# Putting off GpSimd's output sums and softmax weights behind the last low part of a block's input

## The chip, the cores and the metric

The kernel runs on one core of a Trainium2 chip. The metric is the time of one execution on the device, in microseconds (us). The engines are named as in the profile: PE (TensorE) multiplies matrices, ACT (ScalarE), DVE (VectorE) and POOL (GpSimd) work element by element, SP (SyncE) issues the DMAs. Each engine runs its own instructions in the order in which the program issued them, and semaphores order the engines among each other.

## The reference, cut to what matters

The inputs are `x` (8 x 4096 x 192), `weight_gen` (8 x 4096 x 8 heads x 7 taps) and the two weights of a feed-forward layer, `w_in` (192 x 2048) and `w_out` (2048 x 192). All is float32.

```
w = softmax(weight_gen over the 7 taps)
a[s, head, g] = sum over k of w[s, head, k] * x[s - 6 + k, head, g]     (zeros ahead of the sequence)
h = a @ w_in
out = (h * cos(h)) @ w_out
```

So each token gets a weighted sum of its own row and the six rows ahead of it, and that goes through a feed-forward layer whose activation is h times cos(h).

## The kernel before, in words

The 32768 tokens lie as 256 rows on each of the 128 partitions. The work goes in 64 blocks of 4 rows of every partition, 512 tokens a block. One loop over rounds `i` drives everything: 8 rounds to a block (`NPAIR`), and in each one pair of 128-wide chunks of the 2048 hidden columns. A float32 operand is split into a high part, which the matmul takes in its fast float32 form, and a low part in bfloat16, so that several cheap products replace an exact one.

What a round holds, engine by engine:

- PE, in this order: `ffn_in_first(i)` (line 484; the first of its matmuls reads `x_lo` of the block), `ffn_out(i - 6)` (line 625; the output product of an older block, 6 rounds behind), inside it `transpose_row` (lines 457 to 464; it turns one row of `xa` two blocks ahead and lets the result ride in free columns of the output's bank), and `ffn_in_second(i)` (line 503).
- ACT and DVE: for the hidden pair of the round before, ACT takes the whole turns (line 513), DVE the fraction (517), ACT the cosine (521), DVE the product h cos(h) (528); ACT and DVE then split it into high and low parts (539, 545). In every other round ACT copies the output bank to `part` (`evacuate`, line 650).
- POOL: the attention of a later block, as 13 steps: 7 products of x with the weights (`pr` or `xa`, line 356) and 6 sums (`xa`, line 372). The loop issues two steps at the end of a round (three in some rounds below 64). Block b starts when its weights are marked ready and block b - 2 has been transposed, both as the program is issued. Beside it POOL does the softmax's larger parts (lines 217 to 220, 294 to 309), the output sums (lines 666 and 667) and the low part of the transposed input (`split`, line 441).

Rounds are counted here by their remainder by 16, since the softmax works on 8 rows, which is two blocks, and repeats after 16 rounds. Of the block that is computed in rounds 8 to 15 the four rows are transposed in rounds 14 and 15, 0 and 1, 2 and 3, 4 and 5 ahead of it, and in the same way in rounds 6 to 13 for the block of rounds 0 to 7 that follow. After each second round ACT copies `part`, and the next round starts with `split`: ACT makes `x_hi` and `x_b` (437, 440), POOL `x_lo`. So `x_lo` of the last row is issued in round 6 (or 14) and PE reads it first at the start of round 8 (or 0).

The output of a block has two halves of the hidden columns and, in each, two pairs of token tiles (`tp` 0 and 1). The first half's `part` waits in `sums`. When the second half's is copied, in round 3 or 11 for `tp` 0 and in round 5 or 13 for `tp` 1, POOL adds the two (line 666, `part`) and then the two 192-wide columns of the result (line 667, `fin`). `finish` registers the DMA of `fin`, which SP issues three rounds later. SP also carries `traded`, a marker between PE's two groups of products in a round: PE's second group waits for it.

A table `later` holds what is put off: `at(when, do)` appends a call to a round, and the round runs its list after its products and ahead of POOL's attention steps. The softmax writes itself into it: subtraction of the maximum and the exponentials' sums in round 1, the reciprocal of the denominator on DVE in round 4, `weights` (line 300, 128 x 448) in round 5, every 16 rounds.

Of the kernel before, what the change touches and what calls it, by code (L numbers as in the profile page):

```python
# [17 lines left out]
ALU = mybir.AluOpType  # L18
# [26 lines left out]
def tile_softmax_conv_then_cos_ffn(  # L45
# [10 lines left out]
    B, S, D = x.shape  # L56
# [15 lines left out]
    LAG = 6  # L72
# [141 lines left out]
    def add_taps(t, out):  # L214
        three_ = work.tile([P, RW * H, 3], F32, name="three", bufs=1)
        three = three_[:, 0:t.shape[1]]
        nc.gpsimd.tensor_tensor(out=three, in0=t[:, :, 0:3], in1=t[:, :, 3:6], op=ALU.add)
        old = three[:, :, 0]
        for more in (three[:, :, 1], three[:, :, 2], t[:, :, 6]):
            nc.gpsimd.tensor_tensor(out=out, in0=old, in1=more, op=ALU.add)  # L220
            old = out
# [43 lines left out]
    PIECES = 8  # L265
    later = {}

    def softmax_later(i, r0, r1):

        n = (r1 - r0) * H  # L270
        tile_ = work.tile([P, RW * H, K], F32, name="taps")
        top = work.tile([P, RW * H], F32, name="top")
        den = work.tile([P, RW * H], F32, name="den")
        nc.sync.dma_start(out=tile_[:, 0:n].rearrange("p a k -> p (a k)"),
                          in_=g_v[:, :, r0 * H * K:r1 * H * K])
        for b in range(r0 // R, r1 // R):
            taps[b] = tile_.rearrange("p (r h) k -> p r h k", h=H)[:, b * R - r0:(b + 1) * R - r0]

        def at(when, do):
            later.setdefault(i + when, []).append(do)  # L280

        def half(start, c0, c1):
            m = c1 - c0
            t, m1, d = tile_[:, c0:c1], top[:, c0:c1], den[:, c0:c1]
            flat = t.rearrange("p a k -> p (a k)")
            step = m * K // PIECES
            num = []

            def numerators():
                num.append(work.tile([P, RW * H // 2, K], F32, name="num", bufs=1)[:, 0:m])  # L290
                nc.scalar.activation(out=num[0], in_=t, func=AF.Silu, bias=-SHIFT, scale=1.0)

            def exponentials():
                nc.gpsimd.tensor_tensor(out=t, in0=t, in1=num[0], op=ALU.mult)
                add_taps(t, d)
                nc.gpsimd.tensor_scalar(out=d, in0=d, scalar1=-1e-9 * math.exp(-SHIFT), scalar2=TWO_PI,
                                        op0=ALU.add, op1=ALU.mult)

            def weights():
                nc.gpsimd.tensor_tensor(  # L300
                    out=t, in0=t, in1=d.unsqueeze(2).broadcast_to([P, m, K]), op=ALU.mult)
                ready.update(range((r0 + c0 // H) // R, (r0 + c1 // H) // R))

            def piece(k):
                cs = slice(k * step, (k + 1) * step)
                nc.vector.reciprocal(out=flat[:, cs], in_=flat[:, cs])

            at(start, lambda: nc.vector.tensor_reduce(out=m1, in_=t, axis=AX.X, op=ALU.max))
            at(start + 1, lambda: nc.gpsimd.tensor_tensor(
                out=t, in0=t, in1=m1.unsqueeze(2).broadcast_to([P, m, K]), op=ALU.subtract))  # L310
            at(start + 4, numerators)
            at(start + 8, lambda: nc.scalar.activation(out=t, in_=t, func=AF.Silu, bias=SHIFT, scale=-1.0))
            for k in range(PIECES):
                at(start + 9 + k, lambda k=k: piece(k))
            at(start + 9 + PIECES, exponentials)
            at(start + 12 + PIECES, lambda: nc.vector.reciprocal(out=d, in_=d))
            at(start + 13 + PIECES, weights)

        for k, c0 in enumerate(range(0, n, RW * H // 2)):
            half(2 + 16 * k, c0, min(c0 + RW * H // 2, n))  # L320
# [114 lines left out]
    def split(b, t, cs, eng):  # L435
        hi, half, lo = parts_of(b)
        nc.scalar.copy(out=hi[:, :, cs], in_=t)  # L437
        yield
        if eng is nc.gpsimd:
            nc.scalar.copy(out=half[:, :, cs], in_=t)  # L440
        eng.tensor_tensor(  # L441
            out=lo[:, :, cs], in0=t, in1=hi[:, :, cs].bitcast(F32), op=ALU.subtract)
        if eng is not nc.gpsimd:
            yield
            nc.scalar.copy(out=half[:, :, cs], in_=hi[:, :, cs].bitcast(F32))  # L445
# [122 lines left out]
    def evacuate_f32(j):  # L568
        b, m = divmod(j, 2 * R)
        half, m = divmod(m, R)  # L570
        tp, bank = divmod(m, 2)
        if bank == 0:
            return
        acc = accs.pop(j // 2)
        part_ = work.tile([P, 2, CT], F32, name=f"part{half}", bufs=(3 if half == 0 else 2))
        part = part_[:, :, 0:D]
        nc.scalar.copy(out=part, in_=acc[:, :, 0:D])
        if half == 0:
            sums[(b, tp)] = part
            return  # L580
        if tp == 0:
            fin_t = work.tile([P, R, D], F32, name="fin")
            finals[b] = fin_t
        fin = finals[b]
        ts = slice(2 * tp, 2 * tp + 2)
        nc.gpsimd.tensor_tensor(out=fin[:, ts, :], in0=part, in1=sums.pop((b, tp)), op=ALU.add)
        finish(j, b, fin, tp)

    def finish(j, b, fin, tp):
        if tp == 1:  # L590
            def store():
                nc.sync.dma_start(out=o_v[:, :, b * R * D:(b + 1) * R * D],
                                  in_=fin.rearrange("p r d -> p (r d)"))

            stores[j + LATE] = store
            finals.pop(b)
            for pair in range(NPAIR):
                g_parts.pop(b * NPAIR + pair)
# [38 lines left out]
    def evacuate(j):  # L637
        if j < NATIVE:
            return evacuate_f32(j)
        b, m = divmod(j, 2 * R)  # L640
        half, m = divmod(m, R)
        tp, s = divmod(m, 2)
        if s == 0:
            return
        group = j // 2
        acc = accs.pop(group)
        bt = group // R + 2
        part = work.tile([P, 2, CT], F32, name=f"part{half}", bufs=(3 if half == 0 else 2))
        if WHOLE < bt < NB:
            nc.scalar.copy(out=part, in_=acc)  # L650
            r = group % R
            splits.append(split(bt, part[:, :, 2 * D:], slice(r * P, (r + 1) * P), nc.gpsimd))
        else:
            nc.scalar.copy(out=part[:, :, 0:2 * D], in_=acc[:, :, 0:2 * D])
        part = part[:, :, 0:2 * D]
        if half == 0:
            sums[(b, tp)] = part
            return
        if tp == 0:
            fin_t = work.tile([P, R, D], F32, name="fin")  # L660
            finals[b] = fin_t
        fin = finals[b]
        old = sums.pop((b, tp))
        eng = nc.gpsimd
        ts = slice(2 * tp, 2 * tp + 2)
        eng.tensor_tensor(out=part, in0=part, in1=old, op=ALU.add)  # L666
        eng.tensor_tensor(out=fin[:, ts, :], in0=part[:, :, 0:D], in1=part[:, :, D:2 * D],  # L667
                          op=ALU.add)
        finish(j, b, fin, tp)

    def last_half():
# [102 lines left out]
    for n in range(2):  # L774
        nc.tensor.matmul(warm[:, n, :], lhsT=ident, rhs=mix_last[0].rearrange("p r d -> p (r d)")[:, 0:CT],
                         start=True, stop=True, skip_group_check=True)
# [31 lines left out]
    for i in range(N + LAG + 1):  # L808
        b, pair = divmod(i, NPAIR)
        j = i - LAG  # L810
# [17 lines left out]
        def products():  # L828
            if b < NB and pair == 0:
                assert b in transposed  # L830
            if whole is not None and j >= 0:

                ffn_out(j)
                ffn_in_first(i, whole)
            elif j >= N - HALF:
                if j == N - HALF:
                    last_half()
                return
            else:
                if i < N:  # L840
                    ffn_in_first(i, h_now if whole is None else whole)
                if i == LAG:
                    ffn_in_second(i)
                if j >= 0:
                    ffn_out(j)
            if i < N and i != LAG:
                ffn_in_second(i)
            if j in stores:
                stores.pop(j)()
            if j >= 0:  # L850
                evacuate(j)
# [95 lines left out]
```

## Time and profile before

| What | Value |
| --- | --- |
| time, median of 3 runs | 2207.09 us (2206.64 to 2210.22) |
| time of the profiled execution | 2209.54 us |
| its span, first to last instruction | 2207.8 us |
| busy: PE, POOL, DVE, ACT | 98%, 92%, 89%, 86% |
| granted TensorE clock, mean | 0.997 |
| POOL's output sums, line 666 and line 667 | 124 each |
| POOL's weights, line 300, 128 x 448 | 28 |

The span is shorter than the time by what lies ahead of the first and behind the last instruction. In rows of the timeline stand the start, the duration, the engine, the line, the operation with its operands, how many instructions are merged and, in brackets, how long the engine was idle just before and what released it. In rows of the waits stand the waiting engine and line, the releaser, the total in us, the count and the longest. Instructions of one engine can overlap by some hundredths, so distances between starts are used for sums.

### The profile page before, as it was taken

The numbers are of one execution on the slowest core, as the hardware profiler recorded it, in microseconds if no ns is written. First come the engines' busy times: TensorE is split into PE (matmuls) and PEld (weight loads), VectorE is DVE, ScalarE is ACT, GpSimd is POOL, SyncE is SP. The second block draws the span as 40 slices with busy tenths as digits, with TensorE's granted clock in tenths as the row PEclk, the third lists the DMA queues.
The fourth block names the chain that finished last, engine by engine and source line by source line (L and its number), as shares of the span: only waits on it lengthen the run. The fifth ranks groups of instructions, "written<-read, shape, count | busy, mean of one in ns | idle before, by whom it ended". The sixth has DMA issues, their size and how long they took to land.

```text
span 2207.8 us, 60871 instructions
## 1 busy us (share of the span) xinstructions
PE 2154.1 (98%) x26428; PEld 1718.4 (78%) x26428; DVE 1973.9 (89%) x1876; ACT 1904.0 (86%) x2380; POOL 2033.8 (92%) x1587
## 2 busy tenths in 40 slices
PE   6999999999999999999999999999999999999998
PEld 3777787777877777877778787778777777778887
DVE  7788999989999899999989998999998899988887
ACT  6788888888888888888888888888888888888886
POOL 8999999999999999999999999999999999999941
PEclk9999999999999999999999999999999999999999
DMA  7312212112122121122121221221211212212100
GB/s 182 70 27 52 53 34 60 34 44 60 27 60 52 35 51 45 42 52 48 38 52 38 49 60 27 52 55 32 60 44 35 59 37 50 52 29 52 34 9 23
DMA packets 25914, 105.56 MB, mean 48 GB/s; under 512 B 2750, under 2 KB 6838, under 8 KB 25646
## 3 DMA queue, kind: packets, MB, share of 16 engines
q1 hardware_dynamic: 25646, 101.67, 19.5%
q8 instruction: 206, 3.38, 0.7%
q14 instruction: 62, 0.51, 0.1%
HBM read 76.50 MB, written 25.17 MB: 46 GB/s over the span
## 4 chain that ended last, share of the span: by engine, by line
POOL 54%; ACT 16%; PE 15%; DVE 10%; issue 4%; DMA 0%; POOLq 0%; ACTq 0%; SPq 0%; DVEq 0%
POOL xa L372 14%; POOL pr L356 14%; POOL part L666 7%; PE acc L625 7%; DVE turn L517 5%; PE h L503 5%; ACT turn L521 5%; POOL xa L356 4%; POOL fin L667 4%; ACT part L650 4%; ACT turn L513 4%; POOL x_lo L441 4%; DVE h L528 3%; PE h L484 3%; ACT ghi L539 2%
## 5 line engine op out<-in xcount | busy, mean ns | idle before, releaser
L625 PE MATMUL acc<-wo,ghi 64*128 64x384 f32 x7984 | 792.7, 335 | 0.4 <-ACT part L650 0.3
L517 DVE TENSOR_TENSOR turn<-h,turn 128x1024 f32<-128x1024 f32 x512 | 626.3, 1223 | 185.2 <-ACT turn L513 185.1
L625 PEld LDWEIGHTS acc<-wo,ghi 64*128 64x128 f32 x7984 | 721.6, 185 | 35.2 <-ACT part L650 10.9
L372 POOL TENSOR_TENSOR xa<-xa,pr 128x768 f32<-128x768 f32 (+1 forms) x378 | 690.2, 1826 | 0.6
L513 ACT ACTIVATE turn<-h 128x1024 int32<-128x1024 f32 x512 | 526.5, 1028 | 154.7 <-PE h L503 149.7
L521 ACT ACTIVATE turn<-turn 128x1024 f32<-128x1024 f32 x512 | 545.8, 1066 | 117.2 <-DVE turn L517 117.1
L528 DVE SCALAR_TENSOR_TENSOR h<-h,turn 128x1024 f32<-128x1024 f32 x504 | 621.1, 1232 | 28.0 <-ACT turn L521 1.1
L545 DVE TENSOR_TENSOR glo<-h,ghi 128x1024 bf16<-128x1024 f32 x504 | 611.7, 1214 | 2.9 <-POOL wo L204 1.7
L356 POOL TENSOR_TENSOR pr<-xt,taps 128x768 f32<-128x768 f32 (+1 forms) x378 | 579.0, 1532 | 8.8
L539 ACT CAST ghi<-h 128x1024 fp32r<-128x1024 f32 x504 | 510.8, 1013 | 1.9 <-DVE h L528 1.9
L625 PE MATMUL acc<-wo_b,glo 64*128 64x192 bf16 x7856 | 409.6, 243 | 0.0
L625 PEld LDWEIGHTS <-glo 64*128 64x128 bf16 x7984 | 327.2, 94 | 15.1 <-issue 2.4
L666 POOL TENSOR_TENSOR part<-part,part 128x768 f32<-128x768 f32 x124 | 229.2, 1848 | 90.9 <-ACT part L650 64.9
L484 PE MATMUL h<-x_hi,wa_hi 64*128 64x512 f32 x1024 | 303.0, 579 | 1.4 <-ACT x_hi L437 1.4
L503 PE MATMUL h<-x_hi,wa_hi 64*128 64x512 f32 x1024 | 302.6, 579 | 0.1
L650 ACT COPY part<-acc 128x1024 f32<-128x1024 f32 x240 | 239.2, 997 | 0.0
L484 PE MATMUL h<-x_lo,wa_hi 64*128 64x512 bf16 x1024 | 205.1, 388 | 27.0 <-POOL x_lo L441 23.7
L503 PE MATMUL h<-x_hi,wb_hi 64*128 64x512 f32 x1024 | 207.6, 394 | 0.0
L484 PE MATMUL h<-x_b,wa_lo 64*128 64x512 bf16 x1024 | 199.3, 377 | 1.9 <-ACT x_b L445 1.0
L503 PE MATMUL h<-x_lo,wa_hi 64*128 64x512 bf16 x1024 | 199.4, 378 | 0.8
L503 PE MATMUL h<-x_b,wa_lo 64*128 64x512 bf16 x1024 | 199.2, 377 | 0.0
L503 PE MATMUL h<-x_b,wb_lo 64*128 64x512 bf16 x1024 | 199.1, 377 | 0.0
(105 smaller groups left out, 2172.4 us busy)
## 6 DMA issues: line engine op xcount, KB each, us to landing
xt<-in_x_dram SPq DMA_DIRECT2D x62, 960.0 KB, 7.0
out_dram<-fin SPq DMA_DIRECT2D x63, 384.0 KB, 3.4
taps<-in_weight_gen_dram SPq DMA_DIRECT2D x15, 448.0 KB, 4.5
raw<-in_moe_w_out_dram SPq DMA_DIRECT2D x8, 384.0 KB, 4.9
raw<-in_moe_w_in_dram SPq DMA_DIRECT2D x10, 256.0 KB, 7.4
xt<-in_x_dram SPq DMA_DIRECT2D x1, 768.0 KB, 11.5
xt<-in_x_dram SPq DMA_DIRECT2D x1, 540.0 KB, 5.6
raw<-in_moe_w_in_dram SPq DMA_DIRECT2D x4, 128.0 KB, 4.9
```

What stands on the lines that cost most here:

```text
L356: eng.tensor_tensor(out=dst.rearrange("p r (h g) -> p r h g", h=H), in0=xt[:, k + ra:k + rb, :].rearrange("p r (h g) -> p r h g", h=H), in ...
L372: eng.tensor_tensor(out=acc if k < K else xa, in0=acc, in1=old[:, ra:rb], op=ALU.add)
L484: nc.tensor.matmul(h[:, q, :], lhsT=w[rs, chunk(pair, q)], rhs=v[rs, q, :], start=(m == 0), stop=False, skip_group_check=True)
L503: nc.tensor.matmul(h[:, 1 - q, :], lhsT=w[rs, cs], rhs=v[rs, q ^ middle, :], start=False, stop=(m == len(prods) - 1), skip_group_check=True)
L513: nc.scalar.activation(out=t.bitcast(I32), in_=hs[i], func=AF.Identity, bias=0.25, scale=1.0)
L517: nc.vector.tensor_tensor(out=t, in0=hs[i], in1=t.bitcast(I32), op=ALU.subtract)
L521: nc.scalar.activation(out=t, in_=t, func=AF.Sin, bias=SIN_BIAS, scale=SIN_SCALE)
L528: nc.vector.scalar_tensor_tensor(out=g, in0=hs[i], scalar=TWO_PI, in1=turns.pop(i), op0=ALU.mult, op1=ALU.mult)
L539: nc.scalar.copy(out=hi, in_=hs[i])
L545: nc.vector.tensor_tensor(out=lo, in0=hs.pop(i), in1=hi.bitcast(F32), op=ALU.subtract)
L625: nc.tensor.matmul(to, lhsT=g[rs, n, t * P:(t + 1) * P], rhs=w[rs, fc, :], start=(lo == 0 and c == 0 and (whole or s == 0)), stop=(lo == 1 ...
L666: eng.tensor_tensor(out=part, in0=part, in1=old, op=ALU.add)
```

## The change

POOL's two sums for `tp` 1 are no longer issued in the round that copies `part` (round 5 or 13) but through `later` two rounds on (round 7 or 15); those for `tp` 0 stay. The softmax's `weights` move from round 5 to round 6. Nothing is computed otherwise. The DMA of `fin` stays where it was, three rounds behind the copy.

```diff
             at(start + 9 + PIECES, exponentials)
             at(start + 12 + PIECES, lambda: nc.vector.reciprocal(out=d, in_=d))
-            at(start + 13 + PIECES, weights)
+            at(start + 14 + PIECES, weights)
...
         old = sums.pop((b, tp))
         eng = nc.gpsimd
         ts = slice(2 * tp, 2 * tp + 2)
-        eng.tensor_tensor(out=part, in0=part, in1=old, op=ALU.add)
-        eng.tensor_tensor(out=fin[:, ts, :], in0=part[:, :, 0:D], in1=part[:, :, D:2 * D],
-                          op=ALU.add)
+        def add():
+            eng.tensor_tensor(out=part, in0=part, in1=old, op=ALU.add)
+            eng.tensor_tensor(out=fin[:, ts, :], in0=part[:, :, 0:D], in1=part[:, :, D:2 * D],
+                              op=ALU.add)
+        if tp == 1:
+            later.setdefault(j + LAG + 2, []).append(add)
+        else:
+            add()
         finish(j, b, fin, tp)
```

## Prediction, made before the change was run

> **What bounds the kernel now.** I read the page's shares first, then the list of waits, then the timeline around one of the waits that carry the change, and last the rest of its 16 rounds. The fences stand in that order; rounds are counted by their remainder by 16.
>
> ```profile
> PE 2154.1 (98%) x26428; PEld 1718.4 (78%) x26428; DVE 1973.9 (89%) x1876; ACT 1904.0 (86%) x2380; POOL 2033.8 (92%) x1587
> POOL 54%; ACT 16%; PE 15%; DVE 10%; issue 4%; DMA 0%; POOLq 0%; ACTq 0%; SPq 0%; DVEq 0%
> ```
>
> PE is busy nearly throughout, so only its few waits can be won. Yet the chain that ended last lies on POOL for 54%: something of POOL's holds PE.
>
> ```profile
> POOL part L666 <- ACT part L650: 64.9, 33, 5.4
> PE h L484 <- POOL x_lo L441: 23.7, 28, 1.1
> PEld L484 <- DVE glo L545: 7.1, 22, 1.7
> PEld acc L462 <- POOL xa L372: 2.2, 1, 2.2
> ```
>
> The second row is PE's longest wait after the start, and its count, 28, is that of POOL's full-sized weights: one in 16 rounds. The first shows POOL idle at other places, 33 times: it is late at one place and early at another. The last, a wait of the transposes for an unfinished `xa`, has happened once; it comes back below. Now the place, PE's first matmul of rounds 5 to 8, with round 5's second group in between:
>
> ```profile
> 1000.88 0.39 PE L484 MATMUL h<-x_lo,wa_hi 64*128 64x512 bf16 x2
> 1003.67 0.38 PE L503 MATMUL h<-x_lo,wa_hi 64*128 64x512 bf16 x2
> 1005.00 0.39 PE L484 MATMUL h<-x_lo,wa_hi 64*128 64x512 bf16 x2
> ...
> 1009.14 0.39 PE L484 MATMUL h<-x_lo,wa_hi 64*128 64x512 bf16 x2
> ...
> 1014.28 0.39 PE L484 MATMUL h<-x_lo,wa_hi 64*128 64x512 bf16 x2 [0.85 <-POOL x_lo L441]
> ```
>
> Rounds 5 and 6 last 4.12 and 4.14 us, round 7 lasts 5.14: the wait of 0.85 costs 1.01 against a round of 4.13, since matmuls that otherwise overlap across the border are drained too. What held `x_lo` back (POOL), and when its input was there (ACT):
>
> ```profile
> 1004.36 0.99 ACT L650 COPY part<-acc 128x1024 f32<-128x1024 f32 x1
> 1005.86 0.74 POOL L441 TENSOR_TENSOR x_lo<-part,x_hi 128x256 bf16<-128x256 f32 x1
> 1006.56 1.83 POOL L666 TENSOR_TENSOR part<-part,part 128x768 f32<-128x768 f32 x1
> 1007.06 0.42 ACT L437 CAST x_hi<-part 128x256 fp32r<-128x256 f32 x1
> 1008.47 1.01 POOL L667 TENSOR_TENSOR fin<-part 128x384 f32<-128x384 f32 x1
> 1009.44 0.98 POOL L300 TENSOR_TENSOR taps<-taps,den 128x448 f32<-128x448 f32 x1
> 1010.50 1.55 POOL L356 TENSOR_TENSOR xa<-xt,taps 128x768 f32<-128x768 f32 x1
> 1012.00 1.54 POOL L356 TENSOR_TENSOR pr<-xt,taps 128x768 f32<-128x768 f32 x1
> 1013.50 0.73 POOL L441 TENSOR_TENSOR x_lo<-part,x_hi 128x256 bf16<-128x256 f32 x1
> 1014.19 1.55 POOL L356 TENSOR_TENSOR pr<-xt,taps 128x768 f32<-128x768 f32 x1
> 1015.69 1.84 POOL L372 TENSOR_TENSOR xa<-xa,pr 128x768 f32<-128x768 f32 x1
> 1017.61 1.54 POOL L356 TENSOR_TENSOR pr<-xt,taps 128x768 f32<-128x768 f32 x1
> ```
>
> The last row's `x_hi` is there at 1007.06 + 0.42 = 1007.48, but `x_lo` starts at 1013.50, ends at 1014.23, and PE starts 0.05 later. POOL was never idle in between: its queue held the two sums (2.88 from start to start of what follows), the weights (1.06) and two products (3.00).
>
> **The change part by part.** *The wait.* All that stood ahead of `x_lo` in round 5 goes: the sums to round 7, the weights to round 6, and the two products too. A block's attention starts when its weights are marked ready, in program order, and that is now round 6; in round 5 the loop issues no step. So `x_lo` follows the row before it (at POOL's idle time from 1006.56 on) and waits for `x_hi` alone. The delay from ACT's end to POOL's start I take as 0.08, from POOL's next wait for ACT, in the fence below: the copy ends at 1038.43 + 1.00, the sum starts at 1039.51. Then `x_lo` runs at 1007.56 to 1008.3, and PE wants it at 1013.27 (1009.14 + 4.13): 5.0 us in hand. Worth 28 x 1.01 = 28.3 us; the lower bound is the waits alone, 23.7.
>
> *The queue behind.* POOL's work is the same, only later, so the question is who waits for what now comes behind `x_lo`. Moved there are the weights 1.06, two products 3.00 and the sums 2.88: 6.94 in all. `x_lo` itself starts 1013.50 - 1007.56 = 5.94 earlier. So what POOL has left then runs 1.00 later than before, while PE's rounds come 1.01 earlier. The cover is POOL's idle time, and the rows that show it are these:
>
> ```profile
> 1032.35 1.85 POOL L666 TENSOR_TENSOR part<-part,part 128x768 f32<-128x768 f32 x1
> ...
> 1035.24 1.86 POOL L372 TENSOR_TENSOR xa<-xa,pr 128x768 f32<-128x768 f32 x1
> 1037.05 0.74 POOL L441 TENSOR_TENSOR x_lo<-part,x_hi 128x256 bf16<-128x256 f32 x1
> 1038.43 1.00 ACT L650 COPY part<-acc 128x1024 f32<-128x1024 f32 x1
> 1039.51 1.85 POOL L666 TENSOR_TENSOR part<-part,part 128x768 f32<-128x768 f32 x1 [1.71 <-ACT part L650]
> ...
> 1071.36 1.84 POOL L372 TENSOR_TENSOR xa<-xa,pr 128x768 f32<-128x768 f32 x1
> ```
>
> At 1039.51 POOL waited 1.71 for the copy that its sum of `tp` 1 needs. In the new order no sum stands there, and this idle time becomes work.
>
> *The transposes, the new tight place.* PE transposes the first row of `xa` 1.92 us into round 6 or 14 and needs the attention's last sum by then:
>
> ```profile
> 1006.92 0.14 PEld L462 LDWEIGHTS acc<-ident,xa 64*128 64x128 f32 x2
> ...
> 1039.07 0.41 PE L484 MATMUL h<-x_lo,wa_hi 64*128 64x512 bf16 x2
> ...
> 1072.37 0.39 PE L484 MATMUL h<-x_lo,wa_hi 64*128 64x512 bf16 x2
> ```
>
> In round 14 (1039.07): the attention started one round late, so its last sum moves from round 11 to round 12, behind the row's `x_lo`. Before it ended at 1037.10, that is 23.60 after the `x_lo` of 1013.50. Now it comes after those 23.60, the 6.94, one more `x_lo` (0.69, 1013.50 to 1014.19) and a wait of 0.31 for the copy of round 11, in all 31.54 behind 1007.56: 1039.10. The wait: that copy stood two rounds ahead of the one at 1038.43, so it ended at 1031.17, now 1030.16, and POOL may go on at 1030.24. POOL arrives at 1007.56, plus the 18.85 from 1013.50 to this sum at 1032.35, plus weights and sums 3.94, less 0.42 because two products (3.00) now stand for a product and a sum (1014.19 to 1017.61): 1029.93, 0.31 too early. PE transposes at 1039.07 - 1.01 + 1.92 = 1039.98. 0.9 us in hand.
>
> In the next round 6 (1072.37) the last sum now ends at 1071.36 + 1.84, less 5.94, plus 6.94, less the idle 1.71, plus the wait of 0.31: 1072.80. PE transposes at 1072.37 - 1.01 + 1.92 = 1073.28. 0.5 us in hand (before: 1.1). So I cost both at nothing, and name the price if the cover is gone: each 0.1 us beyond it is 2.8 us over 28 periods.
>
> *Does POOL's work still fit?* A period of 16 rounds:
>
> ```profile
> 1047.34:1114.63 67.29, 66.50 (x834) 53.33 (x833) 61.30 (x59) 59.20 (x75) 64.48 (x51) 1.00 0.19 43
> 1055.61 0.40 PE L484 MATMUL h<-x_lo,wa_hi 64*128 64x512 bf16 x2
> 1059.96 0.39 PE L484 MATMUL h<-x_lo,wa_hi 64*128 64x512 bf16 x2
> ```
>
> Without its idle 1.71 POOL needs 67.3 - 1.71 = 65.6, gaps between instructions included. PE's 16 rounds would last 67.3 - 1.01 = 66.3. 0.7 is left, of which the two waits named (for `x_hi` in round 6, for the copy in round 11) take a part. POOL will be busy almost throughout and still not bind. Round 2, at 1055.61, lasts 4.35, 0.22 too long: that is a wait for DVE's `glo` (22 of them, row above), after DVE's reciprocals, and I leave it in.
>
> *SP's queue.* The store of `fin` stays three rounds behind the copy, so it has one round behind the sums in place of three.
>
> ```profile
> 1017.41 0.59 SPq L592 DMA_DIRECT2D out_dram<-fin  x1
> ...
> 1050.43 0.59 SPq L592 DMA_DIRECT2D out_dram<-fin  x1
> ```
>
> The sums end at 1007.56 + 0.69 + 1.06 + 3.00 + 2.9 = 1015.2 in round 7 and, by the same counting from 1039.10 (two products, `x_lo`, a product and a sum, the sums), at 1049.1 in round 15. The stores come at 1016.4 and 1049.4 (1.01 earlier than before). Both are free to go, the second by 0.3. Behind it in SP's queue stands the marker that PE's second group of the next round waits for, and that group starts 2.8 into a round (1003.67 less 1000.88), about 3.8 after the store: a store some us late costs nothing either.
>
> *What else moves.* The weights one round later leave the reciprocal of round 4 further behind, at no cost. `part` and `fin` are held two rounds longer; their buffers come round after 8 rounds or more. The x load goes with the attention's steps, one round later, with five rounds before its first reader. At nothing, all of them.
>
> *A rule against it.* POOL's idle time shrinks, so its work meets more of DVE's. POOL's output sum and DVE's reciprocal as they are:
>
> ```profile
> L666 POOL TENSOR_TENSOR part<-part,part x124: 1807/1849/1882, 119.9 to 2180.5; 128x768 f32<-128x768 f32 x124
> L306 DVE RECIPROCAL taps<-taps x232: 316/493/496, 147.4 to 2061.5; 128x56 f32<-128x56 f32 x112, 128x28 f32<-128x28 f32 x4
> ```
>
> Least and most differ by 4% for the sum, and the reciprocal's median is its most but for 3 ns: neither is stretched by what the other does, so the sum stands. The Trainium skill, SBUF — State Buffer, section "Who interferes with whom", says that some DVE forms and POOL take a shared pair of ports by an exclusive lock, the other blocking for the whole instruction. If it bit here, a blocked piece would wait up to a sum's 1.85; the steady durations say that it does not.
>
> **Sum.** 28 x 1.01 = 28.3 less nothing. The profiled execution took 2209.5 around a span of 2207.8, which becomes 2179.5; the median of the runs, 2207.1, stands 0.1% below that execution. From the median: 2178.8, said as 2179.
>
> **The rivals.** *The wait moves to the transposes in part.* For: 0.5 and 0.9 us are small against 30 us of summed queue, and the same wait is in the list once. Against: each term is a row of the same loop and repeats. With 0.5 too late, 28 x 0.5 = 14 us come back: 2193. Still faster.
>
> *All of it comes back elsewhere: no change.* The stall gave ACT and DVE a rest of 1.01 every 16 rounds, just ahead of the reciprocals' rounds. If they need it, PE waits that long later, 2207. Against it: DVE had caught up before the stall, idle in round 7:
>
> ```profile
> 1010.40 1.23 DVE L517 TENSOR_TENSOR turn<-h,turn 128x1024 f32<-128x1024 f32 x1 [0.39 <-ACT turn L513]
> ```
>
> *Slower: the attention's start slips by another round.* If the steps come to be issued ahead of the weights, they start in round 7, and the last sum in round 14 stands two steps (3.4 us) later: 3.4 - 0.9 = 2.5 of wait for 1.01 won, 28 x 1.5 = 42 us more, 2249. It decides from 0.9 + 1.0 = 1.9 us of delay there, or 1.5 in round 6. Against: the round runs its list ahead of the steps. The Trainium skill, TensorE: Matmul & The Clock Gate, section "Why this matters for your kernels", adds that idle gaps over some 3 us drop the clock; no wait in these rows is as long.
>
> *The change does not do what it says*, `x_lo` held by something else: its only other input came 5.8 us before PE's need, so I give that nothing of its own.
>
> **How the numbers follow.** Full gain 0.70 (2175 to 2184), in part 0.17 (2184 to 2202), no change 0.07, slower 0.06. The range: down to 2173 if the 22 waits of 0.2 to 0.3 vanish too (28.3 + about 6), up to 2195 for a wait of 0.5 to 0.6 at the transposes. Bounded by 0.2% (4.4 us), about what a measurement here can tell from no change: faster 0.87, same 0.07, slower 0.06.
>
> **What would show it.** In the changed profile PE's wait for `x_lo` is gone and round 7 lasts 4.13; POOL's idle ahead of the sum in round 13 is gone; POOL waits some tenths for `x_hi` in round 6, 28 times; its busy share rises to 93%; PE's wait for `xa` stays at one. I am wrong if that last one appears some 28 times, if round 2 grows beyond 4.35, or if SP's wait for `fin` shows behind PE's second group.

## Result and the profile after

The changed kernel takes 2180.91 us (median of 4 runs, 2179.65 to 2181.82) against 2207.98 (2206.64 to 2210.22) for the kernel before: ratio 0.9876, 95% interval 0.9859 to 0.9893. The prediction said 2179, between 2173 and 2195. The kernel before has one run more here than above, so its median moved by 0.9.

The shares, the chain that ended last and the waits after, in the order in which they were shown of before. Lines behind the change have moved by one: the sums are now 667 and 668.

```profile
PE 2147.9 (99%) x26428; PEld 1676.9 (77%) x26428; DVE 1974.5 (91%) x1876; ACT 1903.5 (87%) x2380; POOL 2030.0 (93%) x1587
PE 95%; POOL 2%; DVE 1%; ACT 1%; DMA 0%; issue 0%; SPq 0%; DVEq 0%; ACTq 0%; POOLq 0%
```

```profile
POOL x_lo L441 <- ACT x_hi L437: 45.0, 34, 7.5
POOL part L667 <- ACT part L650: 14.0, 28, 5.4
PEld L484 <- DVE glo L545: 9.3, 29, 1.7
PEld acc L462 <- POOL xa L372: 2.1, 1, 2.1
```

The chain lay on POOL for 54%; now it lies on PE for 95%. PE's wait for `x_lo` has left the list, and POOL waits for `x_hi` in its place: what stood at the end of a queue now stands at its head. The wait of the transposes for `xa` is still one. The same place in the timeline, PE's rounds 6, 7 and 8 and POOL's queue:

```profile
990.84 0.39 PE L484 MATMUL h<-x_lo,wa_hi 64*128 64x512 bf16 x2
993.40 0.73 POOL L441 TENSOR_TENSOR x_lo<-part,x_hi 128x256 bf16<-128x256 f32 x1 [0.70 <-ACT x_hi L437]
994.09 0.97 POOL L300 TENSOR_TENSOR taps<-taps,den 128x448 f32<-128x448 f32 x1
994.97 0.39 PE L484 MATMUL h<-x_lo,wa_hi 64*128 64x512 bf16 x2
...
998.15 1.84 POOL L667 TENSOR_TENSOR part<-part,part 128x768 f32<-128x768 f32 x1
999.10 0.39 PE L484 MATMUL h<-x_lo,wa_hi 64*128 64x512 bf16 x2
```

Round 7 lasts 999.10 - 994.97 = 4.13 in place of 5.14. `x_lo` ends at 994.13, 5.0 ahead of PE. Behind it come the weights, the two products (left out in the fence) and the sums, in the predicted order. A whole period of 16 rounds; the row has its length, the busy time of PE, PEld (PE's weight loads), DVE, ACT and POOL with their instructions, then the granted clock, the DMA share and GB/s:

```profile
965.86:1032.17 66.31, 66.31 (x834) 52.04 (x833) 61.30 (x59) 59.20 (x75) 64.40 (x51) 1.00 0.21 50
```

66.31 in place of 67.29. PE counts as busy in all of it, though its round 2 is still 0.2 too long (below).

### The profile page after: what moved, and what is told of

Read it like the earlier page. It is cut to its first block, busy times and chain, and to the rows that moved or that the text cites. A ratio compares the mean times of both kernels' runs of the same rounds, so it can differ in the third digit from the quotient of the medians.

```text
span 2177.9 us, 60870 instructions
## 1 busy us (share of the span) xinstructions
PE 2147.9 (99%) x26428; PEld 1676.9 (77%) x26428; DVE 1974.5 (91%) x1876; ACT 1903.5 (87%) x2380; POOL 2030.0 (93%) x1587
## 4 chain that ended last, share of the span: by engine, by line
PE 95%; POOL 2%; DVE 1%; ACT 1%; DMA 0%; issue 0%; SPq 0%; DVEq 0%; ACTq 0%; POOLq 0%
PE acc L625 47%; PE h L503 30%; PE h L484 15%; PE acc L462 1%; POOL xa L372 1%; POOL pr L356 1%; PE acc L563 1%; PE h L687 0%; POOL wo L204 0%; PE acc L398 0%; DMA xt<-in_x_dram 0%; DVE pr L356 0%; DMA raw<-in_moe_w_in_dram 0%; DVE h L372 0%; DVE turn L517 0%
## 5 line engine op out<-in xcount | busy, mean ns | idle before, releaser
L625 PE MATMUL acc<-wo,ghi 64*128 64x384 f32 x7984 | 788.2, 335 | 0.4 <-ACT part L650 0.3
L625 PEld LDWEIGHTS acc<-wo,ghi 64*128 64x128 f32 x7984 | 713.1, 185 | 43.7 <-ACT part L650 11.0
L625 PE MATMUL acc<-wo_b,glo 64*128 64x192 bf16 x7856 | 404.7, 242 | 0.0
L625 PEld LDWEIGHTS <-glo 64*128 64x128 bf16 x7984 | 322.5, 94 | 19.4 <-issue 2.9
L484 PE MATMUL h<-x_hi,wa_hi 64*128 64x512 f32 x1024 | 298.3, 579 | 1.1 <-ACT x_hi L437 1.1
L503 PE MATMUL h<-x_hi,wa_hi 64*128 64x512 f32 x1024 | 298.0, 578 | 0.1
L650 ACT COPY part<-acc 128x1024 f32<-128x1024 f32 x240 | 239.0, 996 | 0.0
L441 POOL TENSOR_TENSOR x_lo<-part,x_hi 128x256 bf16<-128x256 f32 x240 | 177.4, 739 | 45.0 <-ACT x_hi L437 45.0
L484 PE MATMUL h<-x_lo,wa_hi 64*128 64x512 bf16 x1024 | 200.7, 388 | 3.9 <-DVE t L157 1.8
L484 PE MATMUL h<-x_b,wa_lo 64*128 64x512 bf16 x1024 | 194.5, 376 | 1.7 <-POOL wa_lo L167 1.0
L503 PE MATMUL h<-x_lo,wa_hi 64*128 64x512 bf16 x1024 | 194.5, 376 | 0.8
L503 PE MATMUL h<-x_b,wb_lo 64*128 64x512 bf16 x1024 | 194.7, 376 | 0.0
```

The lines of the kernel that those rows point to most:

```text
L484: nc.tensor.matmul(h[:, q, :], lhsT=w[rs, chunk(pair, q)], rhs=v[rs, q, :], start=(m == 0), stop=False, skip_group_check=True)
L503: nc.tensor.matmul(h[:, 1 - q, :], lhsT=w[rs, cs], rhs=v[rs, q ^ middle, :], start=False, stop=(m == len(prods) - 1), skip_group_check=True)
L625: nc.tensor.matmul(to, lhsT=g[rs, n, t * P:(t + 1) * P], rhs=w[rs, fc, :], start=(lo == 0 and c == 0 and (whole or s == 0)), stop=(lo == 1 ...
```

## Experiments

**Which part does it?** Three kernels hold one piece of the change each. The rivals were that the attention's later start brought the gain, that only the lengths of the named operations count, and that a small relief comes back.

Sums alone, as a difference to the changed kernel:

```diff
-            at(start + 14 + PIECES, weights)
+            at(start + 13 + PIECES, weights)
```

> Only the sums of the second two tiles are put off by two rounds; the weights stay in round 5, so the attention starts there too. Queue theory (PE waits for the last row's x_lo because of what stands ahead of it in POOL's queue): weights (1.06 us) and two products (3.00) still stand ahead, the sums (2.88) do not. x_lo ends about 1.9 us ahead of PE's need, the wait of 0.85 is gone, every round 7 lasts 4.13: about 2181 us, the same as the whole change. Rival (the gain comes from the attention starting a round later): nothing of it is here, 2208 us and 28 waits for x_lo.

Measured 2182.91, ratio to before 0.988 (0.9865 to 0.9894). Weights alone (the sums as before, `weights` at `start + 14 + PIECES`):

> Only the weights are put off by one round; the sums stay ahead of x_lo. Queue theory: with the weights go the two products, 4.06 us, since the attention starts when the weights are issued; the sums' 2.88 stay. x_lo is some 3 us early, no wait, about 2181 us. POOL then waits longer for the copy of round 11 (about 0.7 us). Rival (what counts is the length of the operations that the change names, 2.88 + 1.06, and the weights' own 1.06 is only just more than the wait of 0.85): x_lo would start 1.06 earlier, about 0.1 to 0.2 us ahead of PE's need, with some waits of 0.1 to 0.3 left, 2181 to 2190.

Measured 2181.65, ratio 0.9875 (0.9858 to 0.9891). The second sum alone, against the kernel before:

```diff
         eng.tensor_tensor(out=part, in0=part, in1=old, op=ALU.add)
-        eng.tensor_tensor(out=fin[:, ts, :], in0=part[:, :, 0:D], in1=part[:, :, D:2 * D],
-                          op=ALU.add)
+        def add():
+            eng.tensor_tensor(out=fin[:, ts, :], in0=part[:, :, 0:D], in1=part[:, :, D:2 * D],
+                              op=ALU.add)
+        if tp == 1:
+            later.setdefault(j + LAG + 2, []).append(add)
+        else:
+            add()
```

> Only the second of the two sums (the one into fin, 0.97 us from start to start) is put off by two rounds, nothing else. Queue theory: x_lo lay 0.91 us behind PE's need with its delay; 0.97 less leaves it at the edge, some hundredths to 0.1 us of wait, round 7 lasts 4.13 to 4.3: 2181 to 2186 us. Rival (a stall that is removed by less than a whole step of the schedule comes back, because POOL restarts from ACT's copy in each block): the wait stays near 0.85, 2200 to 2208.

Measured 2182.09, ratio 0.9877 (0.9863 to 0.9892). All three have the whole gain. In none does PE wait for `x_lo` in the steady rounds. What is left ahead of it in each, from the timelines of sums alone, weights alone and the second sum alone, each with PE's round 8 as its last row:

```profile
991.19 0.74 POOL L441 TENSOR_TENSOR x_lo<-part,x_hi 128x256 bf16<-128x256 f32 x1
991.89 0.98 POOL L300 TENSOR_TENSOR taps<-taps,den 128x448 f32<-128x448 f32 x1
995.95 0.74 POOL L441 TENSOR_TENSOR x_lo<-part,x_hi 128x256 bf16<-128x256 f32 x1
999.72 0.39 PE L484 MATMUL h<-x_lo,wa_hi 64*128 64x512 bf16 x2
```

```profile
995.27 1.83 POOL L666 TENSOR_TENSOR part<-part,part 128x768 f32<-128x768 f32 x1
997.18 1.00 POOL L667 TENSOR_TENSOR fin<-part 128x384 f32<-128x384 f32 x1
998.14 0.74 POOL L441 TENSOR_TENSOR x_lo<-part,x_hi 128x256 bf16<-128x256 f32 x1
1001.65 0.39 PE L484 MATMUL h<-x_lo,wa_hi 64*128 64x512 bf16 x2
```

```profile
992.60 1.84 POOL L666 TENSOR_TENSOR part<-part,part 128x768 f32<-128x768 f32 x1
994.40 0.98 POOL L300 TENSOR_TENSOR taps<-taps,den 128x448 f32<-128x448 f32 x1
998.45 0.74 POOL L441 TENSOR_TENSOR x_lo<-part,x_hi 128x256 bf16<-128x256 f32 x1
999.59 0.39 PE L484 MATMUL h<-x_lo,wa_hi 64*128 64x512 bf16 x2
```

`x_lo` ends 3.0, 2.8 and 0.4 us ahead of PE's need. So neither the attention's start (unmoved in the first and the third) nor any named operation is needed for itself. What counts is whether `x_lo` comes before the need, by however little. The middle fence also refutes the counting by the weights' own 1.06: the two products went with them, or they would stand between the sum at 997.18 and `x_lo`. The third was expected at the edge and has 0.4. Of that 0.1 is the sums' place, 2.88 before and now 992.60 to 994.40 = 1.80, a relief of 1.08 in place of 0.97. The first was expected 1.9 ahead and has 3.0. The expectations took POOL to reach the `x_lo` of the row above at its old place, 0.86 into round 6 (1005.86 less 1005.00). In the traces it starts 0.26 ahead of round 6 in the first kernel, 1.20 into it in the second and 0.57 in the third. With that, and `x_lo` 0.96 too late before (1014.23 less 1013.27), the reliefs of 2.88, 4.06 and 1.08 give 3.04, 2.76 and 0.41 ahead, as measured.

**The tight place.** The prediction said that `xa` now comes late for the transposes if the attention starts another round later. So the weights went to round 7, on top of the change:

```diff
-            at(start + 14 + PIECES, weights)
+            at(start + 15 + PIECES, weights)
```

> The whole change, but the weights in round 7 in place of 6. The attention of the first block starts in round 7 and ends in round 13, with two more steps behind POOL's wait for the copy of round 11. Queue theory: PE's transposes in round 14 then wait 2.4 us for xa, and those of the next round 6 another 1.2 us, since POOL's work from the copy of round 11 to that place is 46.6 us in one piece: 3.6 x 28 = 102 us more than the change, about 2283 (2260 to 2290). Rival (POOL's work is the same, it only has to fit into the period, and 0.9 us are left): 2181.

Measured 2277.09, ratio 1.0309 (1.0294 to 1.0325): slower than before. PE's rounds 14 and 15 and its wait in two periods that follow each other, and the second of them in the next round 6:

```profile
921.93 0.39 PE L484 MATMUL h<-x_lo,wa_hi 64*128 64x512 bf16 x2
926.28 0.14 PEld L462 LDWEIGHTS acc<-ident,xa 64*128 64x128 f32 x2 [2.43 <-POOL xa L372]
930.04 0.39 PE L484 MATMUL h<-x_lo,wa_hi 64*128 64x512 bf16 x2
...
992.25 0.39 PE L484 MATMUL h<-x_lo,wa_hi 64*128 64x512 bf16 x2
996.61 0.14 PEld L462 LDWEIGHTS acc<-ident,xa 64*128 64x128 f32 x2 [2.43 <-POOL xa L372]
998.70 0.39 PE L484 MATMUL h<-x_lo,wa_hi 64*128 64x512 bf16 x2
...
1030.85 0.14 PEld L462 LDWEIGHTS acc<-ident,xa 64*128 64x128 f32 x2 [1.12 <-POOL xa L372]
```

The first wait is 2.43, as worked out (2.4). The second, expected at 1.2 in each period, is 1.12 and comes in every second one. In the others, something else holds PE: round 14 there lasts 8.11, round 14 of the next 6.45. Behind the same wait PE's work took 3.76 and 2.09 us. The granted clock (third value from the end) of these two stretches and of the next such one:

```profile
926.28:930.04 3.76, 3.76 (x31) 2.28 (x32) 1.06 (x2) 0.00 (x0) 3.76 (x4) 0.55 0.00 0
996.61:998.70 2.09, 2.09 (x30) 1.45 (x31) 1.05 (x2) 0.00 (x0) 2.09 (x2) 1.00 0.00 0
1066.20:1070.00 3.80, 3.80 (x32) 2.31 (x34) 1.05 (x2) 0.00 (x0) 3.80 (x4) 0.55 0.00 0
```

After a wait of 2.43 the clock fell to about half in one period of two, for 1.67 us more. Where it fell, PE is late and the second wait does not come. So the total, 96 us over the change, is near the 102 of the expectation in part by luck: about half of the second waits are missing, and the trace has twelve such falls of the clock, some 20 us, which the expectation did not hold.

**What an operation costs, by its place.** One more POOL operation per period, the square of the weights into a tile that nobody reads, behind the weights:

```diff
                     out=t, in0=t, in1=d.unsqueeze(2).broadcast_to([P, m, K]), op=ALU.mult)
                 ready.update(range((r0 + c0 // H) // R, (r0 + c1 // H) // R))
+                for _ in range(1):
+                    more = work.tile([P, RW * H // 2, K], F32, name="more", bufs=1)
+                    nc.gpsimd.tensor_tensor(out=more[:, 0:m], in0=t, in1=t, op=ALU.mult)
```

In the kernel before:

> The kernel before with one more POOL operation per 16 rounds (the square of the weights, 128x448, into a tile that nobody reads; 1.06 us from start to start, as the weights), right behind the weights and so ahead of the last row's x_lo. Queue theory: the wait at round 7 grows by the whole 1.06, to 1.9 us, although POOL is idle 1.7 us elsewhere in the period: 28 x 1.06 = 30 us more, about 2238. Rival (the work only has to fit into the period, and the idle time takes it): 2208.

Measured 2234.11 against 2207.2, ratio 1.0124 (1.0106 to 1.0142). In the changed kernel:

> The whole change with the same additional operation, behind the weights, so behind x_lo. Queue theory: POOL has 0.70 + 0.26 = 0.96 us of idle time per period and xa 0.75 and 1.02 us in hand; the added 1.06 takes these nearly to the end, POOL's period becomes 66.4 against PE's 66.3: 2181 to 2186 us, against 30 us for the same operation in the old place. Rival (the order is as tight as before, every addition shows in full): 2181 + 30 = 2211.

Measured 2182.64, ratio 0.9885 (0.987 to 0.9901). With two of them in the changed kernel:

> The whole change with two such operations, 2.12 us per period. Queue theory: now POOL's work, 65.35 + 2.12 = 67.5, is longer than PE's 66.3, and PE waits for it at the transposes: 28 x 1.2 = 33 us over the change, about 2214 (2208 to 2222), with the wait at the transposes of xa and none for x_lo. Rival (idle time found elsewhere): 2181 to 2190.

Measured 2203.66, ratio 0.9984 (0.9974 to 0.9993). The waits of these three, one row or two of each (lines moved by three):

```profile
PE h L487 <- POOL x_lo L444: 47.6, 28, 2.1
```

```profile
POOL x_lo L444 <- ACT x_hi L440: 28.2, 22, 7.5
POOL part L670 <- ACT part L653: 5.6, 2, 5.4
```

```profile
PEld acc L465 <- POOL xa L375: 31.9, 55, 2.1
977.05:1044.14 67.09, 66.75 (x834) 51.88 (x832) 61.32 (x59) 59.18 (x75) 66.06 (x53) 1.00 0.21 50
```

The same operation costs 27 us in the old order and 1.7 in the new, less than the spread of its runs. In the old one it went into PE's wait, 23.7 before and 47.6 now, though POOL was idle 1.7 us elsewhere in every period. In the new one it came out of POOL's waits, those for `x_hi` (45.0 to 28.2) and those for the copy (14.0 to 5.6). The second operation finds nothing left: POOL runs through, the period is 67.1 in place of 66.31, and PE waits for it at the transposes, twice a period. That is 28 x 0.8 = 22 us; expected was 33. The operation was too dear in the sum. From the timeline of the kernel before with one more:

```profile
1017.94 0.98 POOL L300 TENSOR_TENSOR taps<-taps,den 128x448 f32<-128x448 f32 x1
1019.00 0.94 POOL L305 TENSOR_TENSOR more<-taps 128x448 f32<-128x448 f32 x1
1019.89 1.54 POOL L359 TENSOR_TENSOR xa<-xt,taps 128x768 f32<-128x768 f32 x1
```

The weights' 1.06 from start to start holds a gap ahead of an operation that reads their result. The square has no such reader and takes 0.89. 28 x 0.89 = 25 is what the first experiment shows, to 2 us, and two squares take 1.9 of which 0.96 were idle. That leaves 0.94, where the period grew by 0.78; the difference was not traced.

**What is next.** Of PE's rounds only round 2 is still long, 4.33 (1040.43 to 1044.76). Just ahead of it DVE had the last piece of the reciprocals and the next softmax's maximum in one round. The first row here is from the list of waits:

```profile
PEld acc L625 <- ACT part L650: 11.0, 29, 0.7
1037.08 0.49 DVE L306 RECIPROCAL taps<-taps 128x56 f32<-128x56 f32 x1
1037.49 0.56 DVE L308 TENSOR_REDUCE top<-taps 128x64 f32<-128x448 f32 x1
...
1039.21 1.06 ACT L521 ACTIVATE turn<-turn 128x1024 f32<-128x1024 f32 x1 [0.78 <-DVE turn L517]
1040.43 0.10 PEld L484 LDWEIGHTS <-wa_hi 64*128 64x128 bf16 x2 [0.27 <-DVE glo L545]
1041.22 1.35 PEld L625 LDWEIGHTS acc<-wo,ghi 64*128 64x128 f32 x16 [0.36 <-ACT part L650]
```

The row at 1040.43 names DVE's `glo`, but it cost next to nothing: the weight load of the rounds beside it starts behind the same idle time of 0.26 to 0.28, and round 2 began on time, 4.13 behind round 1. What held PE inside round 2 is the last row. The first output product writes to the bank that ACT's copy (1040.18 + 0.99 = 1041.17) had to leave. ACT was late with that copy because it had waited 0.78 for DVE's fraction, where in other rounds with a copy it waits 0.4.

So the maximum and the subtraction behind it went one round on, on top of the change:

```diff
-            at(start, lambda: nc.vector.tensor_reduce(out=m1, in_=t, axis=AX.X, op=ALU.max))
-            at(start + 1, lambda: nc.gpsimd.tensor_tensor(
+            at(start + 1, lambda: nc.vector.tensor_reduce(out=m1, in_=t, axis=AX.X, op=ALU.max))
+            at(start + 2, lambda: nc.gpsimd.tensor_tensor(
```

> The whole change, and the softmax's maximum on DVE one round later (round 1 in place of 0, where it met the last piece of the reciprocals), its subtraction on POOL in round 2. Theory: round 2 lasts 4.33 in place of 4.13 because DVE has 0.56 us too much in round 0; with the maximum in round 1 it is gone, 26 x 0.2 = 5 us: about 2175.5. Rival (the two rounds' work only moves): 2181, with the long round one later.

Measured 2175.23 (2174.78 to 2175.73), ratio to the kernel before 0.9855 (0.9839 to 0.987). The change itself stands at 0.9876, from another set of runs; the medians differ by 5.7 us and their runs do not overlap. A period of it, and what is left of PE's waits for the copy, 2 in place of 29:

```profile
964.14:1030.27 66.13, 66.13 (x835) 52.13 (x834) 61.46 (x59) 59.20 (x75) 64.33 (x51) 1.00 0.21 50
PEld acc L625 <- ACT part L650: 1.1, 2, 0.7
```

66.13 is 16 rounds of 4.13: in the steady part no round of PE is longer than the others. The rows that named `glo` went too, from 29 to 2. That the maximum's delay reached PE by way of ACT's copy is read from the rows; no run moved the copy alone.

## Why the prediction was right

*The wait.* 28 x 1.01 was the term that carried the sum. The period fell by 0.98, 28 times that is 27.4, and the medians fell by 27.1, with the runs spreading over 2 to 4. The two profiled spans differ by more, 2207.8 - 2177.9 = 29.9. Most of the remainder is one stretch near 130 us, where both kernels wait alike for the transposes of round 22 (rows of before, then of after):

```profile
129.99 0.28 PE L462 MATMUL acc<-ident,xa 64*128 64x64 f32 x2 [1.84 <-POOL xa L372]
130.00:133.75 3.75, 3.75 (x30) 2.39 (x31) 0.73 (x1) 0.00 (x0) 3.67 (x3) 0.54 0.00 0
```

```profile
130.05 0.28 PE L462 MATMUL acc<-ident,xa 64*128 64x64 f32 x2 [1.81 <-POOL xa L372]
130.00:132.14 2.14, 2.09 (x30) 1.45 (x31) 0.83 (x1) 0.00 (x0) 2.14 (x2) 1.00 0.00 0
```

The clock fell to 0.54 in the execution of before and not in that of after: 1.6 us that are not the change's.

*The start of `x_lo`.* Worked out 2.56 into round 6 (1007.56 less 1005.00), measured 993.40 - 990.84 = 2.56.

*The queue behind.* These rows answer to the two terms in hand:

```profile
1016.06 1.85 POOL L667 TENSOR_TENSOR part<-part,part 128x768 f32<-128x768 f32 x1 [0.26 <-ACT part L650]
1022.95 1.85 POOL L372 TENSOR_TENSOR xa<-xa,pr 128x768 f32<-128x768 f32 x1
1025.82 0.14 PEld L462 LDWEIGHTS acc<-ident,xa 64*128 64x128 f32 x2
1056.47 1.84 POOL L372 TENSOR_TENSOR xa<-xa,pr 128x768 f32<-128x768 f32 x1
1059.06 0.14 PEld L462 LDWEIGHTS acc<-ident,xa 64*128 64x128 f32 x2
```

The wait at round 11 is 0.26 (0.31 worked out). The last sums of the two attentions end 1.0 and 0.75 ahead of the transposes (0.9 and 0.5). POOL's work came out a little too large: 66.31 less its waits of 0.70 and 0.26 is 65.35, against 65.6. The order of the terms, and that neither becomes a wait, held.

*SP.* That the store would find its sums done held: in the wait list of SP after, waits of the store for POOL come to 1.8 us in all over the run.

*Round 2.* It stayed at 4.33, as left in, but the prediction had its cause wrong. It put the 0.22 down to the 22 waits for `glo`; PE waited for ACT's copy there, 29 times before as well (`PEld acc L625 <- ACT part L650`, 10.9 us in all). Of the forecast only the low end of the range, 2173, used that reading.

*The rivals.* That the transposes are the tight place, and that the attention's start one round later still makes the kernel slower than before, was shown by the weights in round 7. The price was too small, 2249 against 2277: only the first wait was counted, not the one in round 6 and not the clock. That ACT and DVE need the rest at round 8 did not come true: every round behind it kept its length.

## What to carry to other kernels

A queue in which one operation is awaited and others are not is worth reading as an order of due times: ask for each operation who waits for it and when, and put those that nobody awaits behind those that somebody does. How much is put behind hardly matters once the due time is met; here moving one operation of 0.97 us bought the same as moving 6.9. Idle time of an engine elsewhere in its period does not help an operation that is stuck in the queue, but it decides how far the rest may slip. So before moving work back, follow it to the next place where it is awaited, and add up what is in hand there.

## What the runs showed of the hardware

The granted clock fell to about half behind gaps between PE's matmuls of 1.84 us (kernel before, 0.54 over 3.75 us) and 2.10 us (weights in round 7, where the weight load waited 2.43; 0.55 over 3.76 us). It stayed at 1.00 behind gaps of the same length, 2.11 us in the next period and 1.81 in the kernel after. Each fall cost 1.6 to 1.7 us. The Trainium skill, TensorE: Matmul & The Clock Gate, section "Why this matters for your kernels", sets the limit at gaps of some 3 us; these were shorter, so the prediction's remark that no wait in its rows was as long was no safeguard. The same page, section "What's actually happening", says that the window of 3.4 us runs freely; that the same wait met both outcomes agrees with it.

In the profile POOL starts an operation that reads the result of the one ahead 0.08 us behind its end (1017.94 + 0.98 to 1019.00), and one that does not 0.05 ahead of it (1019.00 + 0.94 to 1019.89). That is a difference of 0.13 us between two orders of the same operations.
